# Gated linear attention and a squared-ReLU layer: scores within chunks of 128 steps, with past steps in a state

## The chip, the cores and the metric

The kernel runs on one core of a Trainium2 chip. The metric is the device time of one launch in microseconds (us), the median of several runs. An engine is called as in the profile: PE multiplies matrices, PEld loads its weights, DVE and ACT work elementwise, POOL (GpSimd) and SP mostly issue DMA transfers here, each from a queue of its own in which order is kept.

## The reference

For each of 4 batches and 8 heads there is a sequence of 768 steps with vectors of 48 elements. The complex gate `a` is scaled to a magnitude of at most 0.999, and a complex state of 48 x 48 is carried from step to step:

```python
for t in range(S):
    new_re = ar * S_re - ai * S_im
    new_im = ar * S_im + ai * S_re
    kv = np.einsum('bhd,bhe->bhde', k[:, :, t], v[:, :, t])
    S_re, S_im = (new_re + kv, new_im)
    y[:, :, t] = np.einsum('bhd,bhde->bhe', q[:, :, t], S_re)
```

The 3072 rows of `y` (batch and step; 8 x 48 = 384 columns) then go through `g = max(x @ w_in, 0) ** 2` with 2048 columns and through `g @ w_out` back to 384 columns. The two weight matrices come as 8-byte floats.

## The kernel before

**Units.** The work is cut into 8 units: a batch and one half of its steps (384). An even unit is the first half of its batch, an odd one ("late") the second half.

**Chain of a unit** (`chain_work`): loads on SP's queue; magnitudes and scaling (`roots`, `normalise`); running products of the gate within three consecutive steps (`inner`), then over the 128 groups of three, which PE turns so that groups lie along the free axis (`totals`, tile `tot`), DVE multiplies up (`scan`, tile `e`) and PE turns back (`back`, tile `bk`, L819). With the running product E of all gates, `apply` makes Q = q E and K~ = k / E, both with a real and an imaginary part (96 elements), in one tile `QK` per half of the heads (index z). In all these tiles a partition p holds the three steps 3p, 3p + 1, 3p + 2. The chain is nearly all DVE and ACT work.

**Pairs of a unit** (`pair_work`): for each of the four pairs of heads, `turn` transposes Q and K~ (tile `tq`, twelve transposes of 128 columns) and ACT copies them in the order of time into `QKT`; `score` multiplies K~ and Q of the unit's 384 steps. The matrix of scores is lower triangular in blocks of 128: three blocks on the diagonal, masked by DVE (L875, L883), and three below it, copied by ACT (L876, L884); tile `A` holds all six. `mix` multiplies the scores by v into `ypair`, the two heads in partitions 0 to 47 and 64 to 111, and ACT copies the result to `yt`, which goes by DMA to `xT`. What a late unit needs of the first half comes from a state `S` per head: `keep` (L898, tile `kv`) sums K~ times v over an even unit's 384 steps, with `vn`, a second copy of v whose partitions hold steps in the order of `QK`; in a late unit `mix` begins with Q times this state (L910).

**The layer**: `hidden` (h, L945; 48 matmuls of 384 columns a unit, then ReLU and square on ACT) and `project` (o, L959; 48 matmuls of 384 columns a unit). An f32 matmul is two passes in the profile, so h and o have 768 passes each. h of a unit needs `xT` of all its pairs.

**Weights.** `convert(i)` loads one of 32 pieces as pairs of 32-bit words on POOL's queue (tile `raw`) and makes f32 of it: one ACT step (L583) and three DVE steps (L585, L591, L594). Pieces 0 to 15 are of w_in, 16 to 31 of w_out. DVE's first step of pieces 4 to 15 is ordered behind unit 0's scan (`mark["scanned"]`), of the w_out pieces behind unit 1's last product in `apply` (`mark["second"]`). At the end `inspect` loads all weights once more (tile `look`) for a check by DVE.

**What sets the order.** A planner at compile time gives every engine a fixed queue. Where several instructions can go, the one that is earlier in the program's text goes first. The text is: chain of unit 0; pairs of unit 0 merged with the conversion of w_in; chain of unit 1 and h of unit 0; pairs of unit 1 merged with the conversion of w_out; chain of unit 2; then a loop over n from 1 to 7 that merges h and o of unit n (for n = 1 also o of unit 0) with the pairs of unit n + 1 and the chain of unit n + 2 (for n = 6 with the 32 inspections). On each engine the instructions run in the order planned, whatever is ready.

**Buffers.** PSUM tiles `tot`, `bk`, `tq` and `kv` share two buffers (pool `trp`); scores have two others (`scp`). `QK` has two buffers, one for each half of the heads; tiles of pool `nat` (a, qk, vn) have one each.

Of the kernel before, what the change touches and what calls it, by code (L numbers as in the profile page):

```python
# [481 lines left out]
def fast_path(ctx, tc, q, k, v, a_re, a_im, moe_w_in, moe_w_out, out, flag):  # L482
# [10 lines left out]
    nc = tc.nc  # L493
# [25 lines left out]
    scp = ctx.enter_context(tc.tile_pool(name="scp", bufs=2, space=PSUM))  # L519
    yp = ctx.enter_context(tc.tile_pool(name="yp", bufs=1, space=PSUM))  # L520
# [16 lines left out]
    mask2 = mask.unsqueeze(1).to_broadcast([C, 2, C])  # L537
# [28 lines left out]
    def convert(i):  # L566

        dst, src = piece(i)
        if not wide:
# [4 lines left out]
        raw = (gp.tile([C, DM, 2], U32, name="raw", tag="g") if i < NF else  # L574
               wst.tile([C, DM, 2], U32, name="raw", tag="raw"))
# [3 lines left out]
        lo, hi = raw[:, :, 0], raw[:, :, 1]  # L579
        bits = dst.bitcast(U32)  # L580

        more = wst.tile([C, DM], U32, name="more", tag="more", bufs=2)
        act.activation(out=more, in_=lo, func=AF.Copy, scale=2.0 ** -29)  # L583

        first = dve.tensor_scalar(out=bits, in0=hi, scalar1=0x07FFFFFF, scalar2=3,  # L585
                                  op0=ALU.bitwise_and, op1=ALU.logical_shift_left)
        if i >= NF:
            after(first, mark["second"])
        elif i >= EARLY:
            after(first, mark["scanned"])  # L590
        dve.scalar_tensor_tensor(out=bits, in0=hi, scalar=0xC0000000, in1=bits,  # L591
                                 op0=ALU.bitwise_and, op1=ALU.bitwise_or)

        dve.tensor_tensor(out=bits, in0=bits, in1=more, op=ALU.add)  # L594

    EARLY = 4
# [18 lines left out]
    def load(u):  # L615
# [21 lines left out]
        if u["half"] < NHALF - 1:  # L637
            u["vn"] = nat.tile([C, H, W, D], F32, name="vn", tag="vn")
            nc.sync.dma_start(out=u["vn"].rearrange("p h c d -> p h (c d)"),
                              in_=src(v).rearrange(LOADS, c=W))  # L640
# [128 lines left out]
    def product(u, dst, x, y):  # L769
# [16 lines left out]
        return dve.tensor_tensor(out=dst[:, 1], in0=f[0][:, 1], in1=f[1][:, 0], op=ALU.add)  # L786

    def scan(u):
# [16 lines left out]
        for m in range(NM):  # L805
            done = product(u, v4[:, :, m, 1:32], v4[:, :, m, 1:32],
                           inc[:, :, m, 0:31].unsqueeze(3).to_broadcast([C, 2, 31, 4]))
        mark.setdefault("scanned", done)
# [14 lines left out]
    def apply(u, z):  # L823
# [15 lines left out]
        t = pr.tile([C, 2, HH, W, 2, D], F32, name="QK", tag="QK")  # L839
        u.setdefault("QK", {})[z] = t  # L840
        for j in range(2):
            for r in range(2):
                done = dve.tensor_tensor(out=t[:, j, :, :, r], in0=qk[:, j], in1=a[:, r],  # L843
                                         op=ALU.mult)
        if u["n"] == 1:
            mark["second"] = done


    def turn(u, i, c):
# [3 lines left out]
        src = u["QK"][2 * i // HH]  # L853
        ps = trp.tile([R, 4, C], F32, name="tq", tag="tr")
        for j in range(2):
            for h in range(2):
                nc.tensor.transpose(  # L857
                    ps[:, 2 * j + h],
                    src[:, j, (2 * i + h) % HH, c].rearrange("p r d -> p (r d)"), ident)
        act.copy(out=u["T"][i].rearrange("r z (p c) -> r c z p", c=W)[:, c], in_=ps)  # L860

    def score(u, i, h):

        T = u["T"][i]
        if h == 0:
            u.setdefault("A", {})[i] = pr.tile([C, 2, 6, C], F32, name="A", tag="A")
        A = u["A"][i]
        if h < 2:
            qt, kt = T[:, h], T[:, 2 + h]
            sa = scp.tile([C, 4, C], F32, name="sa", tag="sc")  # L870
            nc.tensor.matmul(sa[:, 0:3].rearrange("p n t -> p (n t)"), lhsT=kt[:, 0:C],  # L871
# [16 lines left out]
    def keep(u, i):  # L888

        if u["half"] == NHALF - 1:  # L890
            return
        if i == 0:
            state[u["b"]] = wk.tile([R, H, D], F32, name="S", tag="S", bufs=2)
# [200 lines left out]
```

## Time and profile before

| what | value |
|---|---|
| median of 5 runs | 839.82 us (836.85 to 842.63) |
| the profiled execution | 841.0 us |
| its span, first to last instruction | 839.3 us |
| PE busy | 749.1 us, 3090 passes, mean granted clock 0.981 |
| DVE busy | 507.4 us, 1284 instructions |
| ACT busy | 435.5 us |
| DMA | 61.24 MB, mean 73 GB/s |
| last product of `QK` of units 0 to 7 ends at | 67.8, 150.3, 235.5, 302.5, 398.6, 490.9, 579.4, 671.2 us |
| PE stands idle over 1 us after 60 us at | 100.1, 117.0, 130.7, 142.3, 158.7, 215.9, 314.8, 407.9, 682.1 us |

A line of the profile's groups gives the line of the kernel, engine and operation, what it writes and reads, the shapes, and the number of instructions; then busy time and mean duration, and the idle time before them with what ended it. A line of a timeline gives the start and the length of a run of equal instructions, in us from the start of the span, and in brackets the idle time ahead of it and its releaser. PE's busy times overlap, since a pass starts before the one ahead of it has ended; the distance of starts says what a pass takes in a stream. A line of the stretches gives a stretch and its length, then the busy time and number of instructions of PE, PEld, DVE, ACT and POOL, the granted clock of PE as a share of full speed, the busy share of the DMA engines, and GB/s. A line of the DMA issues gives the size of one transfer and the median time from issue to landing.

### The profile page before, as it was taken

What the parts mean: (1) busy time and instruction counts of PE and PEld (TensorE: products, weight loads), DVE (VectorE), ACT (ScalarE), POOL (GpSimd) and SP (SyncE); (2) the same over time, 40 slices, a digit from 0 to 9 for tenths busy, and PEclk for the clock granted to TensorE, in tenths of its full rate; (3) what the DMA queues carried; (4) which work ended last, traced back from release to release, by engine and by line L of the source; (5) the groups of instructions that cost most, each with busy time, mean ns of one, the idle gap of its engine ahead of it and who ended that gap; (6) DMA issues with size and microseconds to landing.
All of it is one profiled execution on the core that took longest, in us unless ns stands there. A gap on an engine that the chain in (4) does not pass through costs nothing.

```text
span 839.3 us, 9088 instructions
## 1 busy us (share of the span) xinstructions
PE 749.1 (89%) x3090; PEld 453.7 (54%) x3090; DVE 507.4 (60%) x1284; ACT 435.5 (52%) x865; POOL 43.6 (5%) x75
## 2 busy tenths in 40 slices
PE   0129995999899899999999999999999989999996
PEld 0016553555466456666566666666666646555553
DVE  5997888889989667168643877187717856200000
ACT  5616883765498149621884259524972234422510
POOL 4101000200000000000000000000000143000000
PEclk9999998999999899999999999999999989999998
DMA  9615301740030151001500150005100378100000
GB/s 287 177 62 167 78 0 29 241 126 20 18 112 8 45 142 27 7 17 34 141 8 8 54 158 8 8 10 155 20 8 17 92 223 278 56 16 27 0 10 23
DMA packets 76920, 61.24 MB, mean 73 GB/s; under 512 B 28736, under 2 KB 71744, under 8 KB 76864
## 3 DMA queue, kind: packets, MB, share of 16 engines
q1 hardware_dynamic: 70720, 35.40, 15.3%
q0 software_dynamic: 6144, 25.17, 9.2%
q8 instruction: 26, 0.43, 0.2%
q14 instruction: 30, 0.25, 0.1%
HBM read 51.12 MB, written 4.72 MB: 67 GB/s over the span
## 4 chain that ended last, share of the span: by engine, by line
PE 58%; DVE 15%; issue 12%; DMA 6%; ACT 5%; POOL 0%; SPq 0%; POOLq 0%; ACTq 0%
PE h L945 20%; PE o L959 19%; PE ypair L914 4%; PE sa L871 4%; PE tq L857 3%; DVE fa L782 3%; PE sb L881 2%; DMA look<-in_moe_w_out_dram 2%; PE kv L898 2%; DVE QK L843 2%; DMA look<-in_moe_w_in_dram 2%; DVE fb L834 1%; ACT QKT L860 1%; PE sa L873 1%; PE ypair L910 1%
## 5 line engine op out<-in xcount | busy, mean ns | idle before, releaser
L945 PE MATMUL h<-xT,w 128*128 128x384 f32 x768 | 274.4, 496 | 8.7 <-DMA xT<-yt 6.7
L959 PE MATMUL o<-w,g 128*128 128x384 f32 x768 | 264.0, 491 | 0.0
L959 PEld LDWEIGHTS o<-w,g 128*128 128x128 f32 x768 | 141.7, 191 | 86.2 <-issue 4.7
L945 PEld LDWEIGHTS h<-xT,w 128*128 128x128 f32 x768 | 139.9, 193 | 87.6 <-DMA xT<-yt 8.9
L860 ACT COPY QKT<-tq 96x512 f32<-96x512 f32 x96 | 80.3, 852 | 48.3 <-PE tq L857 46.1
L950 ACT ACTIVATE g<-h 128x384 f32<-128x384 f32 x128 | 61.8, 488 | 65.2 <-PE h L945 64.7
L857 PE MATMUL tq<-ident,QK 128*96 128x128 f32 x384 | 62.1, 289 | 14.7 <-DVE QK L843 12.7
L857 PEld LDWEIGHTS tq<-ident,QK 128*96 128x96 f32 x384 | 46.3, 133 | 43.0 <-issue 27.0
L951 ACT ACTIVATE g<-g 128x384 f32<-128x384 f32 x128 | 66.5, 524 | 2.4
L875 DVE TENSOR_TENSOR A<-sa,mask 128x256 f32<-128x256 f32 x64 | 26.4, 419 | 58.8 <-PE sa L873 58.5
L782 DVE TENSOR_TENSOR fa<-e 128x192 f32<-128x192 f32 (+1 forms) x56 | 23.8, 455 | 60.0 <-ACT e L755 59.4
L871 PE MATMUL sa<-QKT 96*128 96x384 f32 x128 | 55.4, 515 | 0.6 <-ACT QKT L860 0.6
L914 PE MATMUL ypair<-A,v 128*48 128x256 f32 (+2 forms) x384 | 50.8, 389 | 1.5 <-ACT A L884 1.4
L876 ACT COPY A<-sa 128x256 f32<-128x256 f32 x64 | 23.2, 370 | 53.3 <-DVE A L875 53.3
L843 DVE TENSOR_TENSOR QK<-qk,a 128x576 f32<-128x576 f32 x64 | 44.4, 749 | 0.0
L753 PE MATMUL tot<-ident,last 128*128 128x128 f32 x72 | 14.1, 298 | 31.4 <-ACT last L715 28.7
L1037 DVE TENSOR_SCALAR flag<-cnt 1x1 int32<-1x1 f32 x1 | 0.1, 147 | 69.1 <-PE cnt L1036 69.1
L914 PEld LDWEIGHTS ypair<-A,v 128*48 128x48 f32 x384 | 22.8, 124 | 33.9 <-issue 24.3
L963 ACT COPY ot<-o 128x384 f32<-128x384 f32 x24 | 11.4, 475 | 56.8 <-PE o L959 56.8
L607 POOL DMA_DIRECT2D look<-in_moe_w_in_dram x16 | 12.3, 770 | 508.7 <-DVE A L875 493.1
L884 ACT COPY A<-sb 128x256 f32<-128x256 f32 x32 | 11.7, 366 | 47.1 <-DVE A L883 47.1
L873 PEld LDWEIGHTS sa<-QKT 96*128 96x128 f32 x128 | 24.7, 195 | 17.7 <-issue 2.2
(104 smaller groups left out, 921.9 us busy)
## 6 DMA issues: line engine op xcount, KB each, us to landing
raw<-in_moe_w_in_dram POOLq DMA_DIRECT2D x16, 384.0 KB, 5.2
raw<-in_moe_w_out_dram POOLq DMA_DIRECT2D x16, 384.0 KB, 5.3
look<-in_moe_w_in_dram POOLq DMA_DIRECT2D x16, 384.0 KB, 4.3
look<-in_moe_w_out_dram POOLq DMA_DIRECT2D x16, 384.0 KB, 4.3
a<-in_a_re_dram SPq DMA_DIRECT2D x16, 288.0 KB, 3.1
a<-in_a_im_dram SPq DMA_DIRECT2D x16, 288.0 KB, 3.5
qk<-in_q_dram SPq DMA_DIRECT2D x16, 288.0 KB, 4.7
qk<-in_k_dram SPq DMA_DIRECT2D x16, 288.0 KB, 5.0
```

Of the source, the lines that this page charges most:

```text
L782: dve.tensor_tensor(out=t, in0=x, in1=y[:, j].unsqueeze(1).to_broadcast(shape), op=ALU.mult)
L843: done = dve.tensor_tensor(out=t[:, j, :, :, r], in0=qk[:, j], in1=a[:, r], op=ALU.mult)
L857: nc.tensor.transpose(ps[:, 2 * j + h], src[:, j, (2 * i + h) % HH, c].rearrange("p r d -> p (r d)"), ident)
L860: act.copy(out=u["T"][i].rearrange("r z (p c) -> r c z p", c=W)[:, c], in_=ps)
L871: nc.tensor.matmul(sa[:, 0:3].rearrange("p n t -> p (n t)"), lhsT=kt[:, 0:C], rhs=qt, start=True, stop=True)
L873: nc.tensor.matmul(sa[:, 3], lhsT=kt[:, 2 * C:3 * C], rhs=qt[:, 2 * C:3 * C], start=True, stop=True)
L875: dve.tensor_tensor(out=A[:, h, 0:4:3], in0=sa[:, 0:4:3], in1=mask2, op=ALU.mult)
L914: nc.tensor.matmul(ypair[64 * h:64 * h + D, j * C:L], lhsT=u["v"][:, j, 2 * i + h], rhs=A[:, h, lo:hi].rearrange("p n t -> p (n t)"), star ...
L945: nc.tensor.matmul(ps, lhsT=w1[:, f, m], rhs=u["xT"][:, m], start=(m == 0), stop=(m == NM - 1))
L950: act.activation(out=t, in_=ps, func=AF.Relu)
L951: act.activation(out=t, in_=t, func=AF.Square)
L959: nc.tensor.matmul(u["o"], lhsT=u["g"][f][:, ts(c, C)], rhs=w2[:, f], start=(f == 0), stop=(f == NF - 1))
```

## The change

- **Scores.** Only the three diagonal blocks are made, each by a matmul of 128 columns, and DVE masks the three in one instruction of 384 elements. ACT's copies of the blocks below the diagonal go, and so do the matmuls of 256 columns.
- **State by chunk.** `keep` makes K~ times v for each chunk of 128 steps by itself (three chunks in an even unit, two in a late one) and adds them up: the state before chunk 1, before chunk 2 and, in an even unit, at its end. The first sum of an even unit is a copy by ACT, the others are additions by DVE that read PSUM. `mix` multiplies, for each chunk, the scores by v, and Q by the state before the chunk; both add up in `ypair`.
- **K~ in the order of chunks.** `apply` makes K~ ahead of Q, writes it to memory (`rows`) and reads it back with a partition per step of a chunk (`KC`), two transfers on POOL's queue for each half of the heads. `vn` and its load are gone.
- **Conversion.** The load of a piece is split off (`fetch`); pieces 0 to 7 are fetched right after unit 0's loads and the first four of w_out after them. DVE's first step of w_in's pieces is ordered behind unit 0's last product in `apply`, of w_out's behind unit 1's, with no early ones.
- **Order within a pair**: `keep` comes after the scores instead of after the last turn.

The diff, cut to its core:

```diff
+    mask3 = mask.unsqueeze(1).to_broadcast([C, NM, C])
...
+    def fetch(i):
...
+        raw = raws[i] = (gp.tile([C, DM, 2], U32, name="raw", tag="g") if i < NF else
+                         wst.tile([C, DM, 2], U32, name="raw", tag="raw"))
         get = nc.gpsimd.dma_start(
             out=raw.rearrange("p (m f) two -> p m (f two)", m=src.shape[1]), in_=src)
         after(get, mark["landed"])
...
+    def convert(i):
...
+            after(first, mark["QK", i // NF])
...
+        n = i + (NF // 2 if i < NF else 4)
+        if n < (NF if i < NF else 2 * NF):
+            fetch(n)
...
-        if u["half"] < NHALF - 1:
-            u["vn"] = nat.tile([C, H, W, D], F32, name="vn", tag="vn")
-            nc.sync.dma_start(out=u["vn"].rearrange("p h c d -> p h (c d)"),
-                              in_=src(v).rearrange(LOADS, c=W))
...
+        t = pr.tile([C, 2 * HH * W * R], F32, name="QK", tag="QK")
+        half = HH * W * R
+        out_q = u["Q", z] = t[:, 0:half].rearrange("p (h c e) -> p h c e", h=HH, c=W)
+        out_k = t[:, half:2 * half].rearrange("p (c h e) -> p c h e", h=HH, c=W)
+        u["K", z] = out_k
+        for j, o in ((1, out_k.rearrange("p c h e -> p h c e")), (0, out_q)):
             for r in range(2):
+                done = dve.tensor_tensor(out=o[:, :, :, r * D:(r + 1) * D], in0=qk[:, j],
+                                         in1=a[:, r], op=ALU.mult)
+        mark["QK", u["n"]] = done
+
+        rows = dram.tile([L, HH * R], F32, name="rows", tag=f"rows{z}")
+        kc = u["KC", z] = nat.tile([C, NM, HH, R], F32, name="KC", tag=f"KC{z}")
+        n = NM - u["half"]
+        nc.gpsimd.dma_start(out=rows.rearrange("(p c) e -> p (c e)", c=W),
+                            in_=out_k.rearrange("p c h e -> p (c h e)"))
+        nc.gpsimd.dma_start(out=kc[:, 0:n].rearrange("p j h e -> p j (h e)"),
+                            in_=rows.rearrange("(j p) e -> p j e", p=C)[:, 0:n])
...
     def score(u, i, h):
...
+        sa = scp.tile([C, NM, C], F32, name="sa", tag="sc")
+        for j in range(NM):
+            nc.tensor.matmul(sa[:, j], lhsT=T[:, 2 + h, ts(j, C)], rhs=T[:, h, ts(j, C)],
                              start=True, stop=True)
+        dve.tensor_tensor(out=u["A"][i][:, h], in0=sa, in1=mask3, op=ALU.mult)
...
     def keep(u, i):
...
+        ps = trp.tile([R, NM, 2, D], F32, name="kv", tag="tr")
+        for j in range(n):
+            for h in range(2):
                 hh = 2 * i + h
+                nc.tensor.matmul(ps[:, j, h], lhsT=u["KC", hh // HH][:, j, hh % HH],
+                                 rhs=u["v"][:, j, hh], start=True, stop=True)
+        st = pr.tile([R, 2, 2, D], F32, name="St", tag="St")
+        u.setdefault("S", {})[i] = [total_s if late else None, st[:, 0], st[:, 1]]
+        outs = [st[:, 0], st[:, 1], total_s]
+        before = total_s if late else None
+        for j in range(n):
+            if before is None:
+                act.copy(out=outs[j], in_=ps[:, j])
+            else:
+                dve.tensor_tensor(out=outs[j], in0=ps[:, j], in1=before, op=ALU.add)
+            before = outs[j]

     def mix(u, i):
...
+        for j in range(NM):
+            S_j = u["S"][i][j]
             for h in range(2):
+                nc.tensor.matmul(ypair[64 * h:64 * h + D, ts(j, C)],
+                                 lhsT=u["v"][:, j, 2 * i + h], rhs=A[:, h, j],
+                                 start=True, stop=S_j is None)
             for h in range(2):
+                if S_j is not None:
+                    nc.tensor.matmul(ypair[64 * h:64 * h + D, ts(j, C)], lhsT=S_j[:, h],
+                                     rhs=T[:, h, ts(j, C)], start=False, stop=True)
...
+    for f in w[:1] + [lambda i=i: fetch(i) for i in range(NF // 2)] + w[1:]:
         f()
     merge(pair_work(units[0]), [lambda i=i: convert(i) for i in range(NF)])
+    for i in range(NF, NF + 4):
+        fetch(i)
```

## The prediction

> **What bounds the kernel now.** I read the page first, its busy times and its slices, to see which engine fills which stretch.
>
> ```profile
> PE 749.1 (89%) x3090; PEld 453.7 (54%) x3090; DVE 507.4 (60%) x1284; ACT 435.5 (52%) x865; POOL 43.6 (5%) x75
> ...
> PE   0129995999899899999999999999999989999996
> ...
> DVE  5997888889989667168643877187717856200000
> ```
>
> A slice is 21 us. PE is idle for three slices, DVE is nearly full from the second to the twelfth, and from then on PE is full and DVE is not. The kernel thus has two regimes. The table of stretches, cut where a unit's Q, K~ (tile QK) are finished, says the same: columns are time, then busy time of PE, PEld, DVE, ACT, POOL, then granted clock, DMA share and GB/s.
>
> ```profile
> 150.00:180.00 30.00, 28.45 (x148) 14.96 (x148) 25.44 (x64) 19.90 (x40) 6.48 (x12) 1.00 0.64 212
> 235.00:280.00 45.00, 42.68 (x207) 27.21 (x206) 38.68 (x110) 35.44 (x74) 0.00 (x0) 0.98 0.17 47
> 392.00:484.00 92.00, 90.79 (x406) 57.05 (x405) 54.45 (x137) 52.05 (x106) 0.00 (x0) 1.00 0.19 52
> ```
>
> Where the first regime ends is seen in PE's timeline: the last place in it where PE stands still for DVE is unit 3's transposes back (bk), at 277 us. From there a unit takes 92 us, in which DVE works 54 and PE 91.
>
> ```profile
> 276.87 0.30 PE L819 MATMUL bk<-ident,e 128*128 128x128 f32 x1 [0.39 <-DVE e L785]
> 278.08 0.33 PE L819 MATMUL bk<-ident,e 128*128 128x128 f32 x1 [0.91 <-DVE e L785]
> 279.38 0.48 PE L819 MATMUL bk<-ident,e 128*128 128x128 f32 x1 [0.96 <-DVE e L785]
> ```
>
> So PE work saved ahead of this point only makes PE wait longer there; PE work saved behind it shortens the kernel. Execution and page: 841.0 us, span 839.3; the median of five runs is 839.82 (836.85 to 842.63). I add to the span and give 1.7 us to the rest.
>
> **Prices of PE's passes.** An f32 matmul is two passes. Busy times of passes overlap, so I price by distance between starts:
>
> ```profile
> 429.02 1.50 PE L914 MATMUL ypair<-A,v 128*48 128x384 f32 x12
> 430.46 2.20 PE L945 MATMUL h<-xT,w 128*128 128x384 f32 x6
> 432.50 0.81 PE L871 MATMUL sa<-QKT 96*128 96x384 f32 x2
> 433.14 0.38 PE L873 MATMUL sa<-QKT 96*128 96x128 f32 x2
> 433.36 2.10 PE L945 MATMUL h<-xT,w 128*128 128x384 f32 x6
> ```
>
> A pass of 384 columns takes 0.64/2 = 0.32 us, one of 128 takes 0.22/2 = 0.109, one of 256 takes 0.215 (sb, 438.11 to 438.97 for four). Twelve passes of kv, 48 columns on 96 columns of weights, take 71.38 to 72.44, 0.088 each. The 12 passes of ypair would take 4 x (0.322 + 0.215 + 0.109) = 2.58 us one after the other and take 1.44: the two heads, which write different partitions, run beside each other, 1.29, and changing to them and back adds 0.34 (the h passes around them start later by so much). With the state's four passes (517.62 to 519.70) a late mix takes 2.28 by the same sum.
>
> The change per pair of heads:
> - scores: 2.58 becomes 12 passes of 128, 1.31: **-1.27**.
> - mix of an early unit (even): 1.63 becomes 20 passes of 128, half hidden, 1.09 + 0.34: -0.20. Late unit: 2.28 becomes 24, 1.31 + 0.34 = 1.65: -0.63.
> - kv: six matmuls as before in early units; four new ones in late units, 8 x 0.088 + 0.07 for changing = +0.78.
>
> [...] Here sa's 128-column passes, each with its own 128 columns of weights, start 0.109 us apart, a third of the 384-column ones.
>
> **What of it counts.** I counted PE's instructions behind unit 3's first bk in the two built programs. Scores of 21 pairs: 26.7 us less. Mixes of 22 pairs, 12 late and 10 early: 12 x 0.63 + 10 x 0.20 = 9.6 less. kv: 102 matmuls for 48, 54 x 2 x 0.088 = 9.5 and about 0.9 for changes, 10.4 more. Projection: 313 matmuls for 323, since ten more are placed ahead of it, 6.4 less. Sum: **-32.3 us**.
>
> **When DVE gets to that point** (277 us before):
> - Conversions leave unit 0's chain. Between 13.7 and 63.3 us stood five conversions, each 0.27 + 0.47 + 0.47 = 1.21 us by starts (L585, L591, L594). DVE also waited 1.0 us for raw at 13.67. Part of the chain waits for ACT anyway; I take -5 (bounds -1 and -7).
> - They come back behind unit 0: 16 instead of 11 in its pairs, +6. But DVE stood idle there 6.7 us for PE (0.68, 3.96, 0.64, 1.40), which the change fills, as pairs are shorter. DVE's new work is 16 x 1.21 + 8 masks + 8 adds + the first two steps of the next chain (1.4) = 26.4 us; it had 27.0 from 67.8 to 94.9. A mask of 384 elements is 0.336 x 1.5 = 0.5 (estimate from L875's 256), an add of 96 from PSUM 0.2 (between L782's 48 at 0.2 and 192 at 0.45). With 1 to 2 us of waits I take 0 to +1.
> - K~ through memory: 576 KB written, 576 KB read, both on POOL's queue, the read waiting for the write. The nearest row is vn, which goes away:
>
> ```profile
> vn<-in_v_dram SPq DMA_DIRECT2D x4, 576.0 KB, 4.3
> raw<-in_moe_w_out_dram POOLq DMA_DIRECT2D x16, 384.0 KB, 5.3
> ```
>
> Two such and two issues of 0.6 to 0.8 are 10 us; vn's own slowest, under a full queue, was 17.6, so 10 to 37 for both. K~ is computed ahead of Q, 1.3 us sooner than all is ready. In units 0 and 1 nothing else is queued on PE between the scores and kv: 2.6 us of passes, about 8 with the copies. PE then stands at kv, turn and mix of that unit wait behind it, and on DVE the add waits in front of conversions. I take 0.5 us in unit 0 and 2 in unit 1 (0 to 4 each; more is the third rival).
> - The w_out conversions already waited for raw (1.62, 0.78, 0.84, 0.82); 1.4 MB more in that stretch at its 212 GB/s is 6.6 us of DMA, of which I let 2 through (0 to 6).
> - Masks: three of 0.33 become two of 0.5 and two adds of 0.2, +0.4 a pair in unit 2: +1.5; its waits for PE (2.94, 1.00) shrink: -3.
>
> The four products that make Q and K~ keep 576 elements in runs of 48, so the new order of K~ costs nothing on DVE (L843's 0.67 stays; if the two that write K~ in each half of the heads took twice as long, 2.7 us a unit).
>
> Sum **-5 + 0.5 + 2.5 + 2 - 1.5 = -1.5**; between -8 and +9, as not all bad ends fall together.
>
> **Behind it.** A unit's PE work becomes some 84 us, DVE's 56, so PE stays the bound. New waits: kv's PSUM tile is now freed by DVE's adds, and the second turn after it, one or two groups of passes later (2 to 4 us), needs that tile. Masks in this stretch start 0.5 us (median) and at most 2.5 after their scores, so this mostly fits: +2 in all, 0 to +12. In 665 to 723 us the last checks of the weights ("look") fill the DMA (0.68 busy); 2 MB of K~ more, and adds queued behind looks on DVE: +2 (0 to 5). ACT loses three copies a pair (1.1 us) and gains at most one of 0.24; it hides behind PE, so I cost it at nothing, and if PE did not cover it it would be a gain. The vn loads go from SP's queue, where nothing waited for them.
>
> [...]
>
> Sum: 839.3 - 32.3 - 1.5 + 4 = 809.5, and 1.7: **811 us**. Own range: best 839.3 - 32.3 - 8 + 1.7 = 801; worst 839.3 - 32.3 + 9 + 17 + 1.7 = 835, of which I leave out the last 4.
>
> **Rivals.**
> 1. PE waits for the adds (kv's tile): for it, DVE is in order and also waits for ACT; against it, the short lags above. At 0.8 us for each of 21 keeps behind 277 us, in place of my 2 in all, the kernel is 15 us longer than I say: 826 (817 to 836). Chance 0.15.
> 2. The start shrinks more: PE's shorter pairs remove also the waits of chains 1 and 2, 10 us sooner at the point above, 8.5 sooner than I took, and of the new waits half stay: 811 - 8.5 - 2 = 800. For it, PE waits on DVE at 130.7, 142.3 and 215.9; against it, these show DVE late, not PE. Chance 0.10.
> 3. Slower: K~'s way through memory, from DVE's K~ to kv's operand. The slack is 8 us in units 0 and 1, about 9 in unit 2 (5.8 of passes ahead of its kv), and 15 in units 3 to 7 (12.3 of passes and the copies). A way of 20 us instead of 10 makes 12 + 12 + 11 + 5 x 5 = 60 us of standing, 2.5 of it counted: 811 + 57 = 868. It decides from about 16 us (8 + 8 + 7 + 5 x 1 = 28), where the gain is gone. For it, each read waits for a write, and loads of 2.9 MB start just then; against it, a, q and k landed in at most 8.2 us each. Chance 0.05.
> 4. The short passes do not run at 0.109, or two heads do not overlap at 128 columns: the score and mix gains halve, 811 + 18 = 829. Chance 0.05; against it, ypair's 128-wide passes are in the row above.
>
> My own case: 0.65. The range takes in the first two but for the worst end of each: 799 to 831. Faster by over 0.5% (about what a measurement tells from no change) 0.92, within 0.5% 0.03, slower 0.05: slower is the third rival, and the 0.03 is its beginning, a way of 16 us, out of my own case.
>
> **What would show it.** Right: PE waits 8 to 12 us more ahead of unit 3's bk, which begins at 270 to 280 us; units then take 84 us; sa's passes start 0.109 apart; DVE runs no conversion before 62 us. Wrong: kv idle for DMA in units 2 to 7, turns (tq) idle for DVE's adds, or bk of unit 3 later than 286 us.

## The result and the profile after

The changed kernel takes 844.53 us (median of 25 runs, 840.07 to 854.16), the kernel before in the same series 840.51 (46 runs): ratio 1.0048, interval 1.0031 to 1.0065. It is half a per cent slower; forecast were 811 us and a range of 799 to 831. The profiled execution spans 843.6 us, 4.3 more than that of before.

The page, busy times and slices. PE has less work than before (723 us in place of 749), and yet it is idle more often:

```profile
PE 723.1 (86%) x3474; PEld 467.1 (55%) x3474; DVE 519.5 (62%) x1316; ACT 407.4 (48%) x769; POOL 65.1 (8%) x107
...
PE   0148787599889899999699979999699989999995
...
PEclk9999979599999999999899998999899999999998
```

Slices 4 to 8 (63 to 169 us) show PE at 8, 7, 8, 7, 5 tenths and the granted clock at 7 and 5 in the sixth and eighth; later a 6, 7, 6 and 8 stand in slices 20, 24, 29 and 33, about one for each unit. The stretches that the prediction used say the same: in 392 to 484 us PE is busy 85.04 us in place of 90.79, with more DMA.

```profile
150.00:180.00 30.00, 23.38 (x137) 17.37 (x138) 23.18 (x52) 13.73 (x22) 7.28 (x13) 0.66 0.73 236
235.00:280.00 45.00, 42.69 (x229) 27.91 (x227) 37.48 (x67) 34.74 (x67) 2.64 (x4) 0.96 0.36 112
392.00:484.00 92.00, 85.04 (x431) 55.74 (x430) 54.84 (x140) 47.85 (x93) 2.65 (x4) 0.96 0.23 71
```

Unit 3's first transpose back, where the prediction cut the kernel in two, starts at 295.27 us; before it was 276.87:

```profile
295.27 0.50 PE L822 MATMUL bk<-ident,e 128*128 128x128 f32 x2 [2.22 <-DVE e L789]
```

So the cut serves as the frame of the account. PE's work behind it, by instruction counts in the trace and the prediction's prices, is 528.2 us before and 493.7 after: 34.5 less, by the forecast's own steps 26.9 for scores, 10.7 for mixes, 6.5 for projections placed earlier, and 9.6 more for kv. But PE's idle time there, summed over the gaps in front of its instructions, rose from 10.3 to 26.1 us, and the remainder by 2.7 (of half rate, the trace's list of clock changes has 23.9 us behind the cut, and 13.7 before the change). From the cut to PE's last instruction it takes 538.6 us in place of 554.6, and the end behind that 9.7 in place of 7.8. Sum: +18.4 (the cut) - 34.5 + 15.8 + 2.7 + 1.9 = +4.3. **Two numbers are to be explained: 18.4 us lost ahead of the cut, and 18.5 behind it.**

**Ahead of the cut.** Unit 0's chain ends 5.1 us sooner (62.7 for 67.8), as forecast. Its four pairs then take from 56.0 us (first turn) to 102.1 (last copy of `ypair`), where they took from 59.5 to 96.6 before. PE's timeline tells why. Before the change, the same twelve kv passes take twice as long at 63 us as at 71:

```profile
63.20 2.05 PE L898 MATMUL kv<-vn,QK 128*96 128x48 f32 x12
...
71.38 1.22 PE L898 MATMUL kv<-vn,QK 128*96 128x48 f32 x12
```

PE begins at half rate and comes to full rate at about 70 us. In the changed kernel this takes until 86 us:

```profile
60.05 2.93 PE L882 MATMUL sa<-QKT 96*128 96x128 f32 x12 [0.94 <-ACT QKT L873]
...
73.62 2.93 PE L882 MATMUL sa<-QKT 96*128 96x128 f32 x12
76.34 2.05 PE L899 MATMUL kv<-v,KC 128*96 128x48 f32 x12
...
86.27 1.38 PE L882 MATMUL sa<-QKT 96*128 96x128 f32 x10
...
94.05 1.60 PE L882 MATMUL sa<-QKT 96*128 96x128 f32 x12
```

Twelve score passes of 128 columns take 2.72 us from their first start to that of kv (73.62 to 76.34), 0.23 each, and at 94 us 1.44 (kv starts at 95.49 there), 0.12 each. The row of the granted clock shows nothing of it there (9 in the third and fourth slice, 42 to 84 us); the distance of passes does, and the trace's list of clock changes agrees with it: its first entry, a change to full rate, stands at 70.3 us before and at 86.1 us after. In unit 1 half rate lasts from 151 to 171 us, and there the granted clock shows it (0.66 above); before, it had ended at 149.

**Behind the cut.** The groups of PE's instructions from 300 us to the end, before and after; the last column is the idle time ahead of them and its releaser:

```profile
L945 PE MATMUL h<-xT,w 128*128 128x384 f32 x576 | 203.7, 493 | 5.5 <-DMA xT<-yt 5.3 <-issue 0.3
```

```profile
L953 PE MATMUL h<-xT,w 128*128 128x384 f32 x576 | 208.7, 503 | 19.3 <-DMA xT<-yt 19.3
...
L899 PE MATMUL kv<-v,KC 128*96 128x48 f32 x204 | 19.9, 244 | 0.0
```

kv waits for nothing, but `h` waits 14 us more for `xT`. The timeline around one of these waits:

```profile
397.96 1.43 SPq L632 DMA_DIRECT2D qk<-in_k_dram  x1
399.02 0.55 POOL L856 DMA_DIRECT2D rows<-QK  x1 [1.77 <-DVE QK L849]
...
402.05 0.77 POOL L858 DMA_DIRECT2D KC<-rows  x1 [2.48 <-PE o L967]
...
404.89 0.67 SPq L632 DMA_DIRECT2D qk<-in_k_dram  x1
405.74 0.46 ACT L926 COPY yt<-ypair 112x384 f32<-112x384 f32 x1
406.23 1.28 SPq L934 DMA_DIRECT2D xT<-yt  x2
406.44 0.77 POOL L858 DMA_DIRECT2D KC<-rows  x1 [3.62 <-issue]
...
414.36 2.26 PE L953 MATMUL h<-xT,w 128*128 128x384 f32 x3 [6.09 <-DMA xT<-yt]
```

Everything falls together: unit 4's chain ends, K~ goes to memory and back, the loads of unit 5 start because unit 4's tiles are free, and in their midst unit 3's last `y` (72 KB in each of two transfers) goes to `xT`. Time from issue to landing of these two transfers, before and after:

```profile
DMA to landing us min/median/max: 3.0/3.2/3.4
```

```profile
DMA to landing us min/median/max: 7.4/7.6/7.8
```

At units 3 to 6 the slower of the two took 7.8, 5.6, 7.6 and 5.2 us; before, 3.4, 2.6, 3.4 and 6.6. After waits of 4.3 to 6.1 us the first `h` passes are 0.64 us apart in place of 0.32, for 2.8 to 5.9 us.

By the list half rate began within each of these waits (at 410.4, 505.9 and 598.1 us; they ended at 414.4, 506.9 and 601.4) and lasted 6.8 us each time. A wait of 2.5 us, which ended at 689.8 us, was followed by half rate too (690.2 to 693.7 us by the list).

### The profile page after: what moved, and what is told of

It is laid out like the page before. It is cut to its first block, busy times and chain, and to the rows that moved or that the text cites. A ratio compares the mean times of both kernels' runs of the same rounds, so it can differ in the third digit from the quotient of the medians.

```text
span 843.6 us, 9873 instructions
## 1 busy us (share of the span) xinstructions
PE 723.1 (86%) x3474; PEld 467.1 (55%) x3474; DVE 519.5 (62%) x1316; ACT 407.4 (48%) x769; POOL 65.1 (8%) x107
## 4 chain that ended last, share of the span: by engine, by line
PE 44%; DVE 19%; DMA 11%; issue 3%; ACT 3%; SPq 1%; POOL 0%; ACTq 0%; POOLq 0%
PE h L953 20%; PE o L967 12%; DVE fa L786 5%; DMA a<-in_a_im_dram 3%; PE tq L872 3%; PE sa L882 3%; DMA xT<-yt 2%; PE ypair L918 2%; DMA look<-in_moe_w_in_dram 2%; PE kv L899 2%; DVE QK L849 2%; DMA look<-in_moe_w_out_dram 2%; PE ypair L923 2%; DVE fb L837 1%; DMA KC<-rows 1%
## 5 line engine op out<-in xcount | busy, mean ns | idle before, releaser
L953 PE MATMUL h<-xT,w 128*128 128x384 f32 x768 | 282.4, 507 | 26.5 <-DMA xT<-yt 23.2
L872 PE MATMUL tq<-ident,QK 128*96 128x128 f32 x384 | 65.1, 300 | 25.2 <-DVE QK L849 14.5
L882 PEld LDWEIGHTS sa<-QKT 96*128 96x128 f32 x384 | 54.9, 206 | 16.8 <-ACT QKT L873 4.5
L882 PE MATMUL sa<-QKT 96*128 96x128 f32 x384 | 57.8, 294 | 2.4 <-ACT QKT L873 2.4
L884 DVE TENSOR_TENSOR A<-sa,mask 128x384 f32<-128x384 f32 x64 | 35.0, 551 | 40.2 <-PE sa L882 39.5
L971 ACT COPY ot<-o 128x384 f32<-128x384 f32 x24 | 11.4, 476 | 99.9 <-PE o L967 99.8
L856 POOL DMA_DIRECT2D rows<-QK x16 | 9.2, 573 | 471.6 <-DVE QK L849 305.0
L918 PE MATMUL ypair<-A,v 128*48 128x128 f32 x384 | 42.2, 292 | 0.0
L899 PEld LDWEIGHTS kv<-v,KC 128*96 128x96 f32 x320 | 34.0, 176 | 11.7 <-issue 7.8
L657 ACT ACTIVATE fa<-a 128x1152 f32<-128x1152 f32 x16 | 18.6, 1159 | 39.2 <-DMA a<-in_a_im_dram 39.1
L899 PE MATMUL kv<-v,KC 128*96 128x48 f32 x320 | 33.8, 256 | 4.1 <-DMA KC<-rows 2.7
```

Source lines behind the costliest of these rows:

```text
L872: nc.tensor.transpose(ps[:, 2 * j + h], src, ident)
L882: nc.tensor.matmul(sa[:, j], lhsT=T[:, 2 + h, ts(j, C)], rhs=T[:, h, ts(j, C)], start=True, stop=True)
L884: dve.tensor_tensor(out=u["A"][i][:, h], in0=sa, in1=mask3, op=ALU.mult)
L899: nc.tensor.matmul(ps[:, j, h], lhsT=u["KC", hh // HH][:, j, hh % HH], rhs=u["v"][:, j, hh], start=True, stop=True)
L918: nc.tensor.matmul(ypair[64 * h:64 * h + D, ts(j, C)], lhsT=u["v"][:, j, 2 * i + h], rhs=A[:, h, j], start=True, stop=S_j is None)
L953: nc.tensor.matmul(ps, lhsT=w1[:, f, m], rhs=u["xT"][:, m], start=(m == 0), stop=(m == NM - 1))
```

## The experiments

Theory: PE's half rate makes the front late (CLOCK), and K~'s traffic makes the last `xT` late (TRIP). Rivals: the moved conversions, kv's waits for K~, the order of loads, the chain's latency on DVE and ACT. Times below are the medians of each series; the other columns are of one profiled execution (the fastest of its series in e1, e2, e6, e9 and e18, the slowest in e8, e10, e12, e14 and e16): first `bk` of unit 1 and of unit 3, from the latter to PE's last instruction, and PE's idle time in that.

| kernel | bk unit 1 | bk unit 3 | behind it | idle there | time, us |
|---|---|---|---|---|---|
| before | 130.7 | 276.9 | 554.6 | 10.3 | 840.5 |
| after | 141.4 | 295.3 | 538.6 | 26.1 | 844.5 |
| e1_conv_old | 133.2 | 287.1 | 539.7 | 25.8 | 840.0 |
| e2_conv_new | 131.9 | 276.1 | 548.9 | 10.4 | 838.7 |
| e3_warm | 132.3 | 305.6 | 552.5 | 28.1 | 868.6 |
| e4_carry | 141.6 | 296.9 | 539.8 | 25.5 | 843.6 |
| e5_no_trip | 142.3 | 291.3 | 515.7 | 11.4 | 817.3 |
| e6_warm2 | 131.0 | 282.3 | 538.7 | 26.3 | 839.0 |
| e7_direct | 144.2 | 300.7 | 531.6 | 18.8 | 841.9 |
| e8_loads_late | 143.7 | 296.8 | 528.7 | 19.1 | 833.0 |
| e9_warm_late | 132.2 | 285.8 | 524.4 | 17.0 | 825.1 |
| e10_warm_no_trip | 144.4 | 293.4 | 515.2 | 9.2 | 817.6 |
| e11_vmask | 140.6 | 292.4 | 560.8 | 27.9 | 862.3 |
| e12_vmask_warm | 144.9 | 300.7 | 559.3 | 27.3 | 866.6 |
| e13_hold | 133.7 | 285.0 | 555.2 | 31.2 | 851.1 |
| e14_hold_no_trip | 135.7 | 283.6 | 524.4 | 10.0 | 815.4 |
| e15_hold_late | 133.2 | 284.8 | 538.3 | 16.7 | 838.9 |
| e16_late_carry | 138.8 | 291.7 | 532.1 | 21.2 | 829.6 |
| e17_short_late | 132.7 | 285.6 | 530.3 | 16.2 | 831.2 |
| e18_direct_late | 134.1 | 290.7 | 512.8 | 9.5 | 823.9 |

### One part alone: e1 and e2

e1 takes the changed kernel and puts the conversion back; e2 takes the kernel before and changes the conversion alone.

```diff
 e1 (on after)
-            after(first, mark["QK", i // NF])
+            if i >= NF:
+                after(first, mark["QK", 1])
+            elif i >= 4:
+                after(first, mark["scanned"])
```

e1: 

> The changed kernel with the conversion of the weights as it was before (fetch and convert together, four pieces free, the others of w_in behind unit 0's scan, w_out behind unit 1's last product); scores, states and K~'s way as changed. Theory CLOCK (PE's passes in the pairs of units 0 and 1 start twice as far apart as later, 0.24 us for a score pass of 128 columns in place of 0.11, because the shorter pairs leave PE too empty to leave that state): it stays so here, unit 0's Q, K~ are ready 5 us later as before the change, and unit 3's bk starts at 290 to 302 us; time 840 to 850 us. Theory CONVERSION (16 conversions behind unit 0 in place of 11 delay chain 1): bk of unit 3 is back at 275 to 282 us, time 824 to 832 us.

e2: 

> The kernel before with the changed conversion alone (fetch split off, all pieces behind unit 0's and unit 1's last products); scores of 384 and 256 columns, one state per half, vn. Theory CLOCK: PE's pairs are as full as before, so its passes come to full rate at about 65 us and again at 145, and the start of unit 3's bk is 270 to 278 us; time 833 to 841 us. Theory CONVERSION: bk of unit 3 at 285 us or later, time over 847 us.

e2 cannot be told from before (ratio 0.999, 0.996 to 1.003), and its cut is at 276.1: with the old pairs, the moved conversions cost nothing. e1's cut is at 287.1, 10 us late of before without any moved conversion, and its time is that of before (1.001, 0.998 to 1.004). Unit 0's pairs run at half rate in e1 too, from 60.5 to about 76 us. So neither pure theory holds: the rest of the change alone makes the front 10 us late (2.5 of it at unit 1's `bk`; after that the list has half rate from 135 to 162 us), and the moved conversions add 8 more, all of it ahead of unit 1's `bk`. They cost nothing with the old pairs (e2), nor where the new pairs run at full rate (e6 below, unit 1's `bk` at 131.0). The wait is seen in DVE's queue: in the changed kernel its conversions wait 11.6 us between 62 and 99 us for ACT's step (`more`), which stands on ACT behind copies of `tq` and `kv` that PE delivers late; before, no conversion there waited for ACT.

### Filler products: e3, e6, e13

```diff
+    def warm(u, n):
+        ps = dp.tile([C, L], F32, name="warm", tag="d")
+        for _ in range(n):
+            nc.tensor.matmul(ps, lhsT=ident,
+                             rhs=u["xn"][:, 2].rearrange("p h d -> p (h d)"),
+                             start=True, stop=True)
...
+    warm(units[0], 13)
     merge(pair_work(units[0]), [lambda i=i: convert(i) for i in range(NF)])
...
+    warm(units[1], 15)
     merge(pair_work(units[1]), [lambda i=i: convert(i) for i in range(NF, 2 * NF)])
```

e3: 

> The changed kernel with 13 products of 384 columns into an unused tile behind unit 0's last transposes back and 15 behind unit 1's, where PE stands idle for DVE; they compute nothing that is used. Theory CLOCK: score passes of units 0 and 1 start 0.11 us apart from their first pair on, unit 1's Q, K~ end at about 150 us in place of 159.7, unit 3's bk at 275 to 285 in place of 295, time 825 to 835 us. Theory K~ WAY (the front is late because kv waits for K~ through memory and DVE's adds behind it): passes get shorter but the pairs wait for KC instead, unit 3's bk at 292 us or later, time 842 us or more.

e6: 

> As e3_warm, but unit 1's 15 filler products come behind unit 0's h in the program's text, so they no longer hold h back. Theory CLOCK: unit 0's pairs run at full rate from their first pass, chain 1 is 9 us sooner as it was in e3_warm (unit 1's bk at 132 us in place of 141), unit 1's pairs too, unit 3's bk starts at 277 to 284 us in place of 295, time 826 to 836 us. Rival DVE (from unit 1's chain on DVE and ACT are the bound of the front, so that warm passes in unit 1 gain nothing): unit 3's bk at 285 to 290, time 835 to 841 us.

e13: 

> e6_warm2 with four more filler products of 384 columns in each pair of units 0 and 1 (two behind the turns, two behind the scores; they compute nothing that is used), so that PE does not fall back to half rate within the pairs. Theory CLOCK: no pass of units 0 and 1 behind the first fillers starts at double distance, unit 1's bk at 132 to 136 us and unit 3's bk at 278 to 285 us in every run and not only in some, median 830 to 837 us in place of e6_warm2's 839. Rival: the front is late by DVE's and ACT's work in the pairs (masks of 384, adds, 16 conversions), and full-rate passes only wait longer: unit 3's bk at 290 us or later, 840 us or more.

In e3 unit 1's fillers stood in the text ahead of unit 0's `h` and took it with them: its first `h` starts at 149.6 us. It is 24 us slower and says nothing of the theory beyond unit 1's `bk` at 132.3. e6 mends that. Its timeline:

```profile
49.26 10.83 PE L994 MATMUL warm<-xn,ident 128*128 128x384 f32 x26 [0.57 <-ACT xn L823]
59.92 1.04 PE L872 MATMUL tq<-ident,QK 128*96 128x128 f32 x8
...
63.04 1.60 PE L882 MATMUL sa<-QKT 96*128 96x128 f32 x12 [0.94 <-ACT QKT L873]
```

Seven filler passes are 0.54 to 0.80 us apart, the rest 0.32, so full rate comes 4.5 us after their start (the list has it at 53.7 us), and the first scores run at it (1.60 for 2.93). Unit 1's `bk` is where it was before the change, and the cut 13.0 us sooner, as theory CLOCK had it. The work behind the cut and its length do not change (538.7 and 538.6). In the medians only 5.5 of these 13 us are seen (ratio to before 1.000, 0.997 to 1.003), so the time is in the rival's range and not in the theory's; the profiled execution was the fastest of its ten, 833.3. e10 below shows one way to lose it again. e13 adds four fillers in each pair of units 0 and 1 and holds the rate there as well (no passes at double distance in unit 0's), with the cut at 285.0, but its fillers push 22 projection passes behind the cut (7.1 us), its idle time there is 5.1 us more than in the changed kernel, and at 851.1 us it is slower: a cure that costs more than the illness.

### Without K~'s way: e5, e10, e14, and with half of it: e7

```diff
 e5, e10, e14
-        rows = dram.tile([L, HH * R], F32, name="rows", tag=f"rows{z}")
-        kc = u["KC", z] = nat.tile([C, NM, HH, R], F32, name="KC", tag=f"KC{z}")
...
+        u["KC", z] = out_k
```

```diff
 e7
+        for j in range(n):
+            for c in range(W):
+                p0 = -(-(C * j - c) // W)
+                p1 = -(-(C * (j + 1) - c) // W)
+                d0 = W * p0 + c - C * j
+                nc.gpsimd.dma_start(out=kc[d0:d0 + W * (p1 - p0 - 1) + 1:W, j],
+                                    in_=out_k[p0:p1, c])
```

e5: 

> The changed kernel without K~'s way through memory: the states are summed straight from K~ as DVE wrote it, so K~ of other steps meets v (this part of the computation is changed), with the same matmuls, copies and additions. Theory TRIP (K~'s 1.15 MB written and read in each unit meets the loads of the unit after next and the last xT; without it the DMA engines are done 4 us sooner): xT of the last pair lands 3 to 4 us after its issue at units 3 to 6 in place of 5 to 8, PE's idle time behind unit 3's bk falls from 26 to 10 to 14 us, and time is 826 to 833 us. Rival SCHEDULE (the waits come from the order that the planner wrote and from the chain's latency, whatever the DMA does): idle time behind unit 3's bk stays over 20 us, time 838 us or more. The half-rate passes of units 0 and 1 stay in both.

e10 (e6's fillers added): 

> The changed kernel with the filler products of e6_warm2 and without K~'s way through memory (states summed from K~ of other steps, as in e5_no_trip: this part of the computation is changed). Theory CLOCK plus TRIP: the two account for nearly all of the difference to the forecast of 811 us; unit 3's bk starts at 276 to 284 us, idle time of PE behind it is 10 to 13 us, time 803 to 813 us. If the front has a third cause, unit 3's bk stays at 285 us or later and the time is 815 us or more.

e14 (e13's fillers added): 

> e13_hold without K~'s way through memory (states summed from K~ of other steps, as in e5_no_trip). Theory CLOCK plus TRIP: what e10_warm_no_trip missed was that its passes fell back to half rate at 68 us; with the fillers in the pairs unit 1's bk is at 132 to 136 us, unit 3's at 278 to 284 us, PE's idle time behind it 9 to 13 us, time 801 to 809 us. Rival: unit 3's bk stays at 290 us, time 815 us or more, and the front's delay has another cause than the clock.

e7: 

> The changed kernel with K~ moved from the one place in the chip's memory to the other directly, in nine transfers of 43 partitions for each half of the heads (six in a late unit) in place of a write to and a read from main memory; half the bytes, one latency. Theory TRIP: half of what e5_no_trip gains, time 832 to 840 us, unless the nine issues of some 0.6 us on POOL's queue make KC later than it was (then kv waits for KC, and the time is 845 us or more). Rival SCHEDULE: 842 to 847 us.

e5 is 27 us faster than the changed kernel (ratio to before 0.969, 0.962 to 0.975), more than the 826 to 833 us expected. Behind the cut it saves 22.9 us, with nearly the same passes: 14.7 us are idle time, and most of the rest goes with half rate, of which the list has 3.4 us there in place of 23.9. From 300 us on `h` waits as long as before the change:

```profile
L947 PE MATMUL h<-xT,w 128*128 128x384 f32 x576 | 202.5, 491 | 5.3 <-DMA xT<-yt 5.3
```

This decides for TRIP: kv itself never waited for K~ there, and what K~'s traffic held up was another transfer. The cut stays late in e5 (291.3, 4 us sooner), so the front is another cause. Its last `xT` lands at most 4.4, 3.4, 3.3 and 4.8 us after its issue at units 3 to 6. e10 and e14 confirm the part behind the cut: 515.2, and 524.4 with 8.2 us more of work in it. e10's cut (293.4) and time are those that it expected of a third cause. But its fillers failed, as its timeline shows, so it does not test one:

```profile
63.25 1.57 PE L876 MATMUL sa<-QKT 96*128 96x128 f32 x12
64.66 0.60 PE L866 MATMUL tq<-ident,QK 128*96 128x128 f32 x4
66.20 0.64 PE L866 MATMUL tq<-ident,QK 128*96 128x128 f32 x4 [0.93 <-ACT QKT L867]
67.76 1.09 PE L866 MATMUL tq<-ident,QK 128*96 128x128 f32 x4 [0.92 <-ACT QKT L867]
69.76 2.16 PE L893 MATMUL kv<-v,QK 128*96 128x48 f32 x12 [0.92 <-ACT QKT L867]
```

After two stops of 0.93 us around turns of 0.6 us, PE is at half rate again (from 67.5 us by the list), its pairs last until 106 us, and unit 1's `bk` is at 144.4. The stops alone do not decide it: e6 has the same two, and stays at full rate until 98.1 us.

```profile
67.02 0.64 PE L872 MATMUL tq<-ident,QK 128*96 128x128 f32 x4 [0.96 <-ACT QKT L873]
68.58 0.64 PE L872 MATMUL tq<-ident,QK 128*96 128x128 f32 x4 [0.92 <-ACT QKT L873]
```

In the traces of before and after, the clock changes stand whole multiples of 3.41 us apart. In the step of this length ahead of e10's change PE was busy 52%, in the two steps that hold e6's stops 72 and 73%. But the busy share of a step does not decide alone: before the change, full rate ended after one of 60% (from 275.1 us) and went on after one of 49% (from 135.1 us); after it, full rate went on after one of 44% (from 229.4 us). What decides was not shown.

Over all kernels but e11 and e12, whose sums are others: where passes at double distance filled more than 20 us between 55 and 104 us (after, e4, e5, e7, e8, e10), unit 1's `bk` starts at 141.4 to 144.4; where less than 16, at 130.7 to 135.7, with e16 (11 us, 138.8) between. e14's cut is at 283.6, not at the 277 that would close the account, and its time (815.4) is over the 801 to 809 expected. Of these 6.7 us, 5.0 stand at unit 1's `bk` already (135.7 for 130.7). e7 halves the traffic: 7.0 us less behind the cut, a third of the full gain; its cut is 5.4 us later, and the median falls by 2.6 us, to a time between the two ranges.

### Other order, other cover: e8, e9, e4, e16, e15

```diff
 e8, e9, e15, e16
                     get = nc.sync.dma_start(
                         out=t[:, j].rearrange("p h c d -> p h (c d)"),
...
+                    if ("xT", u["n"] - 2) in mark:
+                        after(get, mark["xT", u["n"] - 2])
```

```diff
 e4, e16
+        lists[0], rest = rest + lists[0], []
+        if n + 1 < NU:
+            lists[0], rest = lists[0][:-3], lists[0][-3:]
```

e8: 

> The changed kernel with the loads of a, q and k of the unit after next put behind the last xT transfer of the unit whose layer comes next, on SP's queue; all transfers stay. Theory ORDER (the last xT is late because 2.3 MB of loads are in the DMA engines ahead of it): the last xT lands 3 us after its issue in place of 5 to 8 and h's waits for it fall from 23 us to under 6; the chain starts up to 8 us later but DVE works only 56 of 92 us; time 828 to 836 us. Rival CHAIN (the chain's latency, loads to bk, sets the period): h's waits go and PE waits for DVE at bk and tq in their place, 842 us or more.

e4: 

> The changed kernel with the last three of the twelve projection parts of each unit (12 products, 7.7 us of PE) put ahead of the next unit's h in the program's text, so that PE has work while the last pair's xT is on its way. Theory XT (of what the shorter pairs save behind 295 us, 6 us in each of units 4, 5 and 6 come back as PE's wait for the last xT transfer, which lands 5 to 8 us after its issue in place of 3, and 2 more as passes at half rate after the wait): waits of h for xT behind 400 us fall from 19 us to under 4, time 822 to 830 us. Rival CHAIN (DVE's chain of the unit after next sets the period; the waits move to bk and tq): h waits fall but PE waits as long at bk or tq for DVE, time 838 to 845 us.

e9: 

> The changed kernel with both the filler products of e6_warm2 and the late loads of e8_loads_late. If the front (half-rate passes, 5.5 us in e6_warm2's median) and the back (loads ahead of the last xT, 11.5 us in e8_loads_late's) are two causes, they add: 844.5 - 17 = 828 us, 823 to 832. If they are one (a late front that moves everything behind it against the loads), it gains no more than the better of the two: 832 us or more.

e16: 

> e9_warm_late with the last three projection parts of each unit put ahead of the next unit's h, as in e4_carry. In e4_carry the waits of h for xT only moved to scores waiting for ACT's copies behind loads that were late; with the loads behind xT ACT's copies come first. Theory XT: h's remaining waits of 3 to 4 us in units 3 to 6 and the half-rate passes behind them go, 813 to 820 us. Rival ACT (ACT's queue holds the copies behind activations that wait for the loads): the waits move to scores and turns again, 823 us or more.

e15: 

> e9_warm_late (825 us) with the fillers within the pairs of units 0 and 1. Theory CLOCK: it keeps e9_warm_late's gain in every run, 820 to 826 us. Rival: e9_warm_late was at full rate already, and the added fillers cost 2 to 6 us: 827 to 831 us.

e8 saves 9.9 us behind the cut, time 833.0 (0.988, 0.984 to 0.992). Its last `xT` of unit 3 still lands 6.6 to 7.0 us after its issue, at 411.8, now together with K~'s read at 411.2, so the loads were one part of the crowd and K~ another; the forecast of waits under 6 us was too good, 15.3 stay from 300 us on. e9 adds the fillers, and both gains hold together, two causes and not one: 825.1, ratio 0.9845 (0.981 to 0.988). e4 is the instructive miss: `h` no longer waits at all, and nothing is won:

```profile
L953 PE MATMUL h<-xT,w 128*128 128x384 f32 x576 | 205.1, 497 | 0.0
L872 PE MATMUL tq<-ident,QK 128*96 128x128 f32 x240 | 36.7, 276 | 6.9 <-DVE St L909 6.9
L882 PE MATMUL sa<-QKT 96*128 96x128 f32 x240 | 35.4, 285 | 10.1 <-ACT QKT L873 10.1
...
L822 PE MATMUL bk<-ident,e 128*128 128x128 f32 x26 | 6.7, 307 | 6.9 <-DVE e L789 6.9
```

Of its idle time 10.1 us are now scores waiting for ACT's copy of `tq`: ACT's queue holds them behind its first step of the next chain, which waits for the loads of `a`. The late DMA reaches PE by another engine; its rival, a chain that sets the period, is in the 6.9 at `bk` as well. e16 does the same on top of e9 and comes to 829.6, no better than e9: from the cut on `h` waits no longer, but `bk` waits 7.0 us, turns 5.8 and scores 5.3, much as its rival had it. e15 (838.9, over both of its ranges) shows again that fillers within the pairs cost more than they bring.

### Another sum by chunk: e11, e12

```diff
+        for h in range(2):
+            hh = 2 * i + h
+            for c in range(W):
+                nc.tensor.matmul(ps[:, h, 0:n].rearrange("p j d -> p (j d)"),
+                                 lhsT=u["KC", hh // HH][:, c, hh % HH],
+                                 rhs=vm[i % 2][:, h, c, 0:n].rearrange("p j d -> p (j d)"),
+                                 start=(c == 0), stop=(c == W - 1))
```

e11: 

> The changed kernel with another way to sums by chunk: K~ stays as DVE wrote it, and a copy of v, loaded from the input in the same order with one block of 48 columns per chunk and zeros elsewhere, is multiplied by it (six matmuls of 144 columns for a pair of an even unit, of 96 in a late one). No transfer waits for K~ any more. Theory TRIP: as e5_no_trip (817 us) plus 0.4 to 0.6 us of PE for each of 21 pairs behind unit 3's bk, some 10 us, of which part falls into waits: 820 to 830 us. Rival: the small transfers of v (43 partitions of two heads) crowd POOL's queue in units 0 and 1, kv waits for them, bk of unit 3 comes later than 300 us and the time is 835 us or more.

e12: 

> e11_vmask with the filler products of e6_warm2. Theory CLOCK: 6 to 12 us less than e11_vmask, 812 to 822 us, and the best of the kernels that compute the same as the reference. Rival: units 0 and 1 are then held by the loads of v, and it is within 3 us of e11_vmask.

Both fail: each is over 30 us above its theory's range. e11's rival had the time (835 us or more), but its cut is at 292.4 and not over 300. PE's work behind the cut is some 14 us more than in the changed kernel (9.9 by counts, of which 4.5 for projections placed later, and 4 to 5 for kv passes of 144 columns, 0.123 us apart in place of 0.085), half rate there lasts 37.6 us in e11 in place of 23.9, `h` waits 15.9 us for `xT` in e11 from the cut on, and turns 11.5 for DVE's additions. No transfer waits for K~, but 36 small transfers of v a unit (24 in a late one) take their place. That they are what crowds `xT` here was not tested by itself.

### The best version: e17, e18

e17 is e9 with 9 and 11 fillers; e18 is e17 with e7's direct transfers.

e17: 

> e9_warm_late with fewer filler products, 9 and 11 in place of 13 and 15: in e9_warm_late they ran 4 us past the point where unit 0's first turn could start and 3 us in unit 1. Theory CLOCK: the shorter run still takes the passes to full rate (that needed 8 us of products in e6_warm2) and wins the overrun back, unit 3's bk at 276 to 283 us, 818 to 824 us. Rival: it is too short, unit 0's pairs run at half rate, unit 3's bk at 290 us or later, 828 us or more.

e18: 

> e17_short_late with K~ moved directly as in e7_direct. Of the waits that the late loads left, the last xT stood behind the read of K~ (both landed at 411 us in e8_loads_late). Theory TRIP: half of those bytes, h's waits fall from 3 to 4 us to 1 to 2, and it is 4 to 8 us less than e17_short_late. Rival: the nine issues on POOL's queue take 4.5 us for each half, as long as the write that they replace, so kv waits more and it is within 2 us of e17_short_late, or slower.

e17's cut (285.6) is e9's, and its time is 6 us more: the shorter fillers won nothing. In e6 full rate had come after 4.5 us of products, not 8. The rival's time came (828 or more), not its cut, and half rate only in part (65.2 to 72.1 us). Behind the cut the list has 20.4 us at half rate in its profiled execution and 6.8 in e9's, so differences of this size between these kernels are not explained by their edits. e18 computes what the reference asks and is the fastest such kernel here, with e9: 823.9 us, ratio to before 0.981 (0.975 to 0.987), 7.3 us below e17 as TRIP had it. From 300 us on its `h` hardly waits:

```profile
L960 PE MATMUL h<-xT,w 128*128 128x384 f32 x576 | 201.0, 489 | 3.6 <-DMA xT<-yt 3.4 <-ACT g L965 0.2
```

## Why the prediction was wrong

- **Right: what PE saves.** -32.3 forecast, -34.5 counted, and passes at the forecast price where PE was at full rate (0.109 for 128 columns; six scores from 418.41 to 419.07 us are 0.11 apart). The fourth rival did not come.
- **Right: unit 0's chain** 5 us sooner (5.1), and K~'s way as a latency: write 4.7 and read 6.8 us by median (5.4 in a late unit), 8.7 to 14.5 from the write's issue to the read's landing, 10 forecast, and under the 16 from which the third rival decides. The third rival did not come; kv waited 2.7 us for K~ in all.
- **Wrong: the sum to unit 3's `bk`, -1.5 us; it was +18.4.** A `bk` later than 286 us was one of its own signs of being wrong. The step that failed is "DVE stood idle there 6.7 us for PE, which the change fills, as pairs are shorter". The pairs of unit 0 became 9 us longer. DVE's waits for PE did go (7.7 us from 62 to 99 us before, none after), but 11.6 us of waits for ACT came in their place, and ACT waited for PE's slow turns. PE's prices came from rows at full rate (kv's from 71.38 us, the others from behind 400); the row of before at 63.20 us, twelve kv passes in 2.05 us in place of 1.22, showed that PE was at half rate where this step stood, and it was not used. Before, half rate ended at 70.3 us, after the change at 86.1; that the wider passes of before made this difference was not shown; what was tested are the fillers (e6, full rate at 53.7 us). Of the 18.4, 10.7 stand at unit 1's `bk` and 7.7 arise from there to unit 3's. The fillers take away 10.4 of the first and 2.6 of the second (e6, profiled execution); without K~'s way 5.0 of the second go and none of the first (e5, where unit 1's `bk` is 0.9 us later). The moved conversions, which cost nothing in e2, take 8.2 of the first (e1), which overlaps with what the fillers win, as unit 0's half rate ended nine us sooner in e1 (77.1 for 86.1 by the list).
- **Wrong: "New waits" behind it, +4; it was 15.8 of idle time and 2.7 more.** The two waits that it named, kv's tile and the looks, were 1.4 us for the additions (`St`), where the first rival had 15, and at most 1.9 at the end. The one that came was not on its list. The prediction treated K~'s way as time that kv waits, and asked what its 1.15 MB hold up only where w_out is loaded and at the looks; in units 3 to 6 it meets the next loads and the last `xT`. Taking the trip away gives 22.9 us back (e5), more than the 18.5.
- What stays open: e14 with both causes removed has its cut at 283.6, not 277, and 815.4 us, not 811; the fillers' own time is in it, but how much of the 5.0 us at unit 1's `bk` is theirs was not separated. Why half rate comes back in some executions and not in others could not be settled from one trace of each.

## What to carry to other kernels

Price a step with rows from its own stretch: the same kv passes took 2.05 us at 63 us and 1.22 at 71, and with the shorter pairs PE stayed at half rate until 86.1 us in place of 70.3. Ask of every added transfer not only who waits for it, but which other transfer is in the air at that time, and who waits for that one. Where a wait is covered by other work and the time does not move (e4), look for the same late transfer in the next engine's queue before the theory is dropped.

## What the runs showed of the hardware

- A stream without a stop did not by itself bring full rate: from 73.62 to 79.2 us PE of the changed kernel ran passes of 128 and 48 columns without a stop and stayed at half rate (until 86.1 us); in e6 full rate came after 4.5 us of 384-column passes. After the waits for `xT` it took 2.8 to 5.9 us. Whether the width of the passes makes the difference was not tested by itself.
- Two stops of 0.93 us, 1.6 us apart, were followed by half rate in e10, and the same two in e6 (0.96 and 0.92) were not. In the traces of before and after, the clock changed only at whole multiples of 3.41 us from its first change.
- At unit 3 two transfers of 72 KB took 3.0 to 3.4 us from issue to landing behind 2.3 MB of loads, 7.4 to 7.8 with K~'s traffic added, and 4.0 to 4.4 in e5, where that traffic alone is left out. Issued on SP's queue, they were late by traffic on POOL's.
